# Attention's first chunks in another order: the first r.k group in y's banks, masks ahead of scaling, u's sums one chunk ahead for a while

## The chip, the cores and the metric

The kernel runs on one core of a Trainium2 chip. The metric is device time in microseconds (us) of one execution. The engines of the core run beside each other, each in its own order, and wait for each other by semaphores: TensorE (PE), VectorE (DVE), ScalarE (ACT), GpSimd (POOL) and SyncE (SP), which issues the DMAs.

## What is computed

Three stages follow each other: a linear attention with decay, a mixture of eight experts with a capacity per expert, and a dense MLP with a squared ReLU. The change is in the first stage alone.

```python
def _attn_ref(r, k, v, w, u):            # (4, 8, 768, 48) each; w, u (8, 48)
    state = np.zeros((B, H, D, D))
    for t in range(S):
        kt, vt, rt = (k[:, :, t], v[:, :, t], r[:, :, t])
        cur = np.einsum('bhd,bhe->bhde', u[None] * kt, vt)
        y[:, :, t] = np.einsum('bhd,bhde->bhe', rt, state + cur)
        state = w[None, :, :, None] * state + np.einsum('bhd,bhe->bhde', kt, vt)
    return y

def reference(...):
    x = attention(r, k, v, w, u)         # as 3072 rows of 384
    x = moe(x, w_gate, w1, w2)           # greedy assignment by logit, 384 rows for each expert
    return relu(x @ w_in) ** 2 @ w_out
```

## The kernel before

Attention works on 24 chunks of 128 tokens: chunk n is tokens 128*(n//4) and on of batch n%4, all eight heads at once. So the first four chunks (n < B, B = 4) have no state behind them, and the last four (n >= NCH - B) leave none.

For each chunk two inputs are loaded, `rk` (r and k with channels on partitions, 448 KB) and `tk` (v and k with tokens on partitions, 392 KB). Then these steps follow; each has a function of its name:

- `prep(n)`, line 212, DVE: scales r and k in place by powers of w.
- `prep_rk(n)`, line 216: pr = r*k, on POOL or (argument V) on DVE.
- `ruk(n)`, line 222, PE: eight small products of pr and u, the weight of each token's own term. `ccput(n)`, line 227, DVE: copies that into cc. For most chunks there is no `ruk`; its products ride along in `logits` (line 284) and `ccput` reads them from there.
- `diagonal(n)`, lines 232 and 235, POOL and ACT: makes the matrices AM with cc on the diagonal and zero elsewhere (the masks).
- `qk(n)`, line 246, PE: the products r.k of a chunk, 32 in the trace, into the banks pA0 and pA1. `am(n, s)`, line 250, DVE: copies those above the diagonal into AM by a predicate.
- `state_y` (line 259, from chunk 4 on) and `chunk_y` (line 266), PE: y = r.state + AM.v into the banks pY0 and pY1; `yev`, ACT, copies y out.
- `kvm` (line 326), PE, with `prep_kk` (line 239, POOL) ahead of it: the chunk's part of the state, in bank pk; `tput` adds it.
- `logits(n, m)`, lines 283 and 284, PE: gate logits of chunk n, and in the same bank u's sums of chunk m, so it reads pr of chunk m. `lev`, `by_token`, `logits_by_token`, `lput`, `xput` bring logits and y to tokens and write y to xd in DRAM by DMA.

PSUM has eight banks, one for each of pA0, pA1, pY0, pY1, pk, pt, pl, pm. A second `qk` thus waits until both `am` of the first have read pA. The pr and cc tiles have two buffers, AM three, rk eight and tk six. `unread(n)` issues n products of ones that nobody reads.

Attention is recorded under a manual schedule: each engine gets its instructions in the order in which the code is written. One pass of the loop over n issues the loads of later chunks, `qk(n + 1)`, `am(n + 1)`, y of chunk n and the logits of chunk n - 1. `R.step` and `R.pace` put in pieces of the later routing, from chunk 8 on. In front of the loop a prologue (lines 365 to 386) starts chunks 0 to 3.

Of the kernel before, what the change touches and what calls it, by code (L numbers as in the profile page):

```python
# [25 lines left out]
FT = mybir.dt.float32  # L26
# [8 lines left out]
B, H, S, D = 4, 8, 768, 48  # L35
C = 128
NC = S // C
NCH = B * NC
# [23 lines left out]
def narrow(nc, t, make):  # L62

    if t.dtype != I32:
        return t, []
    V = nc.vector
    low, high, c = t[:, :, 0], t[:, :, 1], []

    def first():
        c.append(make())  # L70
        V.tensor_scalar(c[0], high, 5, 2, op0=OP.logical_shift_left, op1=OP.logical_shift_right)

    return high.bitcast(FT), [
        first,
        lambda: V.scalar_tensor_tensor(c[0], low, 29, c[0], op0=OP.logical_shift_right, op1=OP.bitwise_or),
        lambda: V.scalar_tensor_tensor(high, high, -1073741824, c[0], op0=OP.bitwise_and, op1=OP.bitwise_or)]
# [8 lines left out]
def attention(ctx, tc, a, R, L, xd):  # L85
# [5 lines left out]
    V, G, A_, PE = nc.vector, nc.gpsimd, nc.scalar, nc.tensor  # L91
# [3 lines left out]
    ps = ctx.enter_context(tc.tile_pool(name="aps", bufs=1, space=bass.MemoryType.PSUM))  # L95
# [7 lines left out]
    def load_rk(n):  # L103
        if n < NCH and n not in RK:
            RK[n] = ld.tile([112, 2, 4, 128], FT, name="rk", bufs=8)
            nc.sync.dma_start(flat(RK[n]), a["rk"][n])

    def load_tk(n):
        if n < NCH and n not in TK:
            TK[n] = ld.tile([128, 784], FT, name="tk", bufs=6)  # L110
            nc.sync.dma_start(TK[n], a["tk"][n])
# [26 lines left out]
    def unread(n, name="pt"):  # L138
        trash = ps.tile([128, 512], FT, name=name)
        for _ in range(n):  # L140
            PE.matmul(trash, R.ones, R.warm, start=True, stop=True)
# [55 lines left out]
    def decays_by_token():  # L197
        pt = ps.tile([128, 4, 112], FT, name="pt")
        for i in range(4):
            PE.transpose(pt[:, i, :], TT[:, i, :], ident[:112, :112])  # L200
        kt = KT[:, :384].rearrange("p (i s d) -> p i s d", i=4, s=2)
        for s in range(2):
            A_.activation(kt[:, :, s, :], pt[:, :, half(s)], AF.Copy)


    pr, cc, kks, pA, AM, pYs, pk, pts, pls, lts, pms, tTs = ({} for _ in range(12))

    def v_of(n, h):
        return TK[n][:, 48 * h:48 * h + 64]

    def prep(n):
        V.tensor_tensor(flat(RK[n]), flat(RK[n]), flat(WRK), op=OP.mult)

    def prep_rk(n, eng=G):
        pr[n] = wk.tile([112, 4, 128], FT, name="pr")
        eng.tensor_tensor(pr[n], RK[n][:, 0], RK[n][:, 1], op=OP.mult)

    def ruk(n):

        p = ps.tile([128, 2, 4], FT, name="pm")  # L220
        for i in range(4):
            PE.matmul(p[:, i // 2], pr[n][:, i], Uw[:, i, :4], start=not i, stop=i == 3, skip_group_check=True)
        ccput(n, p)

    def ccput(n, p):
        cc[n] = wk.tile([128, 2, 4], FT, name="cc")
        V.tensor_copy(cc[n], p)

    def diagonal(n):

        AM[n] = wk.tile([128, 4, 2, 128], FT, name="AM", bufs=3)
        G.affine_select(AM[n][:, :2].rearrange("p i s t -> p (i s) t"), cc[n][:, 0, :, None].to_broadcast([128, 4, 128]),
                        pattern=[[0, 4], [1, 128]], compare_op=OP.is_equal, fill=0.0, base=0, channel_multiplier=-1)
        for h in range(4):
            A_.activation(AM[n][:, 2 + h // 2, h % 2], ident, AF.Copy, scale=cc[n][:, 1, h:h + 1])

    def prep_kk(n):
        kks[n] = wk.tile([128, 400], FT, name="kk")
        G.tensor_tensor(kks[n], TK[n][:, 384:784], KT, op=OP.mult)

    def qk(n):
        pA[n] = [ps.tile([128, 4, 128], FT, name=f"pA{s}") for s in range(2)]
        for i in range(4):
            for c in range(2):
                for s in range(2):
                    PE.matmul(pA[n][s][half(c, 64), i], RK[n][half(s), 1, i, 64 * c:64 * c + 64],  # L246
                              RK[n][half(s), 0, i], start=True, stop=True)

    def am(n, s):
        V.copy_predicated(AM[n][:, :, s], mask[:, None, :].to_broadcast([128, 4, 128]), pA[n][s])  # L250
# [11 lines left out]
    def chunk_y(n):  # L262
        c, b = divmod(n, B)
        for i in range(4):
            for s in range(2):
                PE.matmul(pYs[n][s][half(i % 2, 64), i // 2], v_of(n, 2 * i + s), AM[n][:, i, s],  # L266
                          start=not c and i < 2, stop=True, skip_group_check=True)
# [8 lines left out]
    def logits(n, m):  # L276


        p = pls[n] = ps.tile([128, 128], FT, name="pl")
        q = lambda k: p[32 * k:32 * k + 32]  # L280
        for j in range(2):
            for s in range(2):
                PE.matmul(q(2 * s), wg[:, s, j], YT[n % LATE][:, s, j], start=not j, stop=bool(j), skip_group_check=True)  # L283
                PE.matmul(q(2 * s + 1), Uw[:, 2 * s + j], pr[m][:, 2 * s + j], start=not j, stop=bool(j), skip_group_check=True)

    def lev(n):
        lts[n] = wk.tile([128, 128], FT, name="lts")
        A_.activation(lts[n], pls[n], AF.Copy)
# [28 lines left out]
    def kvm(n):  # L317

        c, b = divmod(n, B)
        if c == NC - 1:  # L320
            return
        p = pk[n] = ps.tile([128, 4, 64], FT, name="pk")
        for i in range(4):
            for s in range(2):
                h = 2 * i + s
                PE.matmul(p[half(s, 64), i], kks[n][:, 48 * h:48 * h + 64], v_of(n, h), start=not i, stop=True,  # L326
                          skip_group_check=True)
# [7 lines left out]
    def tput(n):  # L335
        c, b = divmod(n, B)
        if c == 0:
            A_.activation(T[b], pk[n][:112], AF.Copy)
        elif c < NC - 1:
            V.tensor_tensor(T[b], tTs[n], pk[n][:112], op=OP.add)  # L340
# [8 lines left out]
    def early(i):  # L349
        if 0 <= i < NEARLY:  # L350
            tiles[i], todo = narrow(nc, tiles[i], lambda: wk.tile([128, 384], I32, name="c32", bufs=1))
            for f in todo:
                f()
# [10 lines left out]
    ok = lambda n: 0 <= n < NCH  # L364
# [2 lines left out]
    prep(0)  # L367
    prep_rk(0, V)
    prep(1)
    qk(0)  # L370
    ruk(0)
    prep_rk(1, V)
    diagonal(0)
    prep(2)
    unread(2)
    ruk(1)
    decays_by_token()
    unread(3, "pk")
    am(0, 0)
    am(0, 1)  # L380
    diagonal(1)
    prep_rk(2)
    prep_kk(0)
    load_rk(5)
    load_tk(3)
    prep(3)
    for n in range(NCH):
        load_rk(n + AHEAD_RK)
        load_tk(n + AHEAD_TK)
        if n == NCH - B:  # L390
            R.cnt0 = ps.tile([128, 512], FT, name="pk")
        if ok(n - 2):
            lput(n - 2)
            if n - 2 < NCH - LATE:
                xput(n - 2)
            if ok(n + 2):
                ccput(n + 2, pms[n - 2].rearrange("p (s e) -> p s e", s=2)[:, :, 32:36])
        elif n == 1:
            ruk(3)
        if ok(n + 3) and n != 1:  # L400
            prep_rk(n + 3)
        if ok(n + 2) and n:
            diagonal(n + 2)
        if n + 1 < NCH - B:
            prep_kk(n + 1)
        R.pace(n - 1)
        R.step(wide=False)
        fade(n)
        if ok(n + 1):
            qk(n + 1)  # L410
        if ok(n + 4) and n:
            prep(n + 4)
        R.step(wide=False)
        if ok(n + 1):
            am(n + 1, 0)
            R.step(wide=False)
            am(n + 1, 1)
        early(n - NCH + NEARLY)
        R.step(wide=False)
        state_y(n)  # L420
        if ok(n - 1):
            logits(n - 1, min(n + 3, NCH - 1))
            lev(n - 1)
        chunk_y(n)
        yev(n, 0)
        yev(n, 1, None if n < NCH - 1 else V)
        early_split(n - 1 - NCH + NEARLY)
        early_load(n + 2 - NCH + NEARLY)
        kvm(n)
        if n == 0:  # L430
            prep(4)
            ruk(2)
            prep_rk(4, V)
            diagonal(2)
        tput(n)
        if n >= NCH - B:
            R.flush()
        if ok(n - 1):
            if n - 1 < NCH - LATE:
                by_token(n - 1)  # L440
            logits_by_token(n - 1)
        R.step(4)
    n = NCH - 1
    early_split(NEARLY - 1)
    lput(n - 1)
    p = ps.tile([128, E], FT, name="pl")
# [827 lines left out]
```

## Time and profile before

| what | us |
|---|---|
| median of three runs | 792.2 (791.05 to 792.97) |
| the profiled execution | 794.57 |
| its span, first to last instruction | 792.7 |
| PE busy in the span | 764.3 (96%) |
| DVE, ACT, POOL busy | 416.6, 379.3, 301.3 |

A row of the timeline gives the start in us from the span's start, the duration, engine, line, operation, out<-in, shapes and count, and in brackets the idle time of the engine before it with what ended it ("issue" where the profile shows nothing). A row of the windows gives for each engine the busy time in the window and the number of instructions, then the granted clock of TensorE (1.00 is 2.4 GHz, 0.50 is 1.2 GHz), the mean busy share of the 16 DMA engines, and GB/s. In the trace one fp32 product of the program is two weight loads (PEld) and two matmuls (PE), and a transpose one of each.

### The profile page before, as it was taken

To read this page: it belongs to the slowest core of one execution; us is meant where nothing else is said; L and a number is where in the kernel's file an instruction comes from. 1 tells how busy PE (TensorE), PEld (TensorE's weight loads), DVE (VectorE), ACT (ScalarE), POOL (GpSimd) and SP (SyncE) were. 2 spreads that over 40 slices of the span, in tenths; PEclk is the share of its full clock that TensorE was granted. 3 is DMA by queue.
4 is the path that set the end of the run, shared out by engine and by line. 5 is a ranking of instruction groups with operands and counts; after the bars stand their busy time and mean duration, and the time that the engine had idled before them with its cause. 6 is when DMAs were issued, how large, how long until landed. Compare 5 with 4: busy or idle time off the path is not lost.

```text
span 792.7 us, 16726 instructions
## 1 busy us (share of the span) xinstructions
PE 764.3 (96%) x6442; PEld 720.8 (91%) x6443; DVE 416.6 (53%) x1082; ACT 379.3 (48%) x886; POOL 301.3 (38%) x321
## 2 busy tenths in 40 slices
PE   8899997799999999999999999999999999999996
PEld 5688885598999999999999999999999999999996
DVE  8679998988974562356235623562355113212210
ACT  3556661446563464346434643464346445443542
POOL 6879842676754060406040604060406072113001
PEclk8999996899999999999999999999999999999999
DMA  9988761674351050105010501050105042101000
GB/s 212 263 242 255 234 203 55 184 242 143 100 173 47 1 170 1 51 1 170 1 50 1 170 1 50 1 170 1 51 1 170 1 132 58 31 16 35 1 1 30
DMA packets 36591, 73.74 MB, mean 93 GB/s; under 512 B 4657, under 2 KB 24353, under 8 KB 36513
## 3 DMA queue, kind: packets, MB, share of 16 engines
q1 hardware_dynamic: 33440, 63.25, 27.4%
q0 software_dynamic: 3072, 9.44, 3.6%
q8 instruction: 50, 0.82, 0.4%
q14 instruction: 29, 0.23, 0.1%
HBM read 63.24 MB, written 9.44 MB: 92 GB/s over the span
## 4 chain that ended last, share of the span: by engine, by line
PE 86%; DVE 6%; DMA 2%; issue 2%; POOL 1%; ACT 1%; SPq 1%; POOLq 0%; DVEq 0%; ACTq 0%
PE acc L907 12%; PE ph L907 12%; PE acc L909 12%; PE acc L908 12%; PE ph L908 11%; PE ph L909 11%; PE pA L246 3%; PE pY L266 3%; DMA raw<-in_w_dram 2%; PE ph L1033 1%; PE pl L283 1%; PE pt L303 1%; PE pk L326 1%; PE pY L259 1%; PE misc L714 1%
## 5 line engine op out<-in xcount | busy, mean ns | idle before, releaser
L904 POOL TENSOR_TENSOR wl<-raw,wh 128x384 fp32r<-128x384 f32 x114 | 116.0, 1033 | 182.7 <-ACT wh L903 150.8
L1084 DVE TENSOR_TENSOR al<-ph,ah 128x384 fp32r<-128x384 f32 x105 | 58.5, 557 | 148.1 <-ACT ph L1078 146.5
L907 PE MATMUL ph<-YH,wi 128*128 128x384 f32 x384 | 132.7, 346 | 0.0
L908 PE MATMUL ph<-YL,wi 128*128 128x384 f32 x384 | 129.4, 337 | 1.2 <-DVE YL L1057 1.2
L907 PE MATMUL acc<-wo,ah 128*128 128x384 f32 x384 | 130.2, 339 | 0.0
L909 PE MATMUL acc<-wo,al 128*128 128x384 f32 x384 | 128.9, 336 | 0.7 <-POOL al L1084 0.7
L1071 ACT ACTIVATE t<-ph 128x384 f32<-128x384 f32 x128 | 61.6, 487 | 141.5 <-PE ph L909 132.2
L909 PE MATMUL ph<-YH,wi 128*128 128x384 f32 x384 | 128.9, 336 | 0.0
L908 PE MATMUL acc<-wo,ah 128*128 128x384 f32 x384 | 128.6, 335 | 0.0
L1099 POOL DMA_INDIRECT out_dram<-rows,idx x24 | 23.7, 987 | 212.3 <-ACT rows L1097 208.0
L903 ACT ACTIVATE wh<-raw 128x384 fp32r<-128x384 f32 x128 | 66.1, 523 | 72.0 <-DMA raw<-in_w_dram 22.4
L1041 DVE SCALAR_TENSOR_TENSOR al<-ph,ah 128x384 fp32r<-128x384 f32 x64 | 35.6, 556 | 86.7 <-ACT ah L1040 80.1
L908 PEld LDWEIGHTS ph<-YL,wi 128*128 128x128 f32 x384 | 72.2, 188 | 2.2 <-DVE YL L1057 2.0
L909 PEld LDWEIGHTS acc<-wo,al 128*128 128x128 f32 x384 | 72.1, 188 | 1.4 <-POOL al L1084 1.0
L907 PEld LDWEIGHTS ph<-YH,wi 128*128 128x128 f32 x384 | 72.3, 188 | 0.0
L908 PEld LDWEIGHTS acc<-wo,ah 128*128 128x128 f32 x384 | 72.2, 188 | 0.0
L907 PEld LDWEIGHTS acc<-wo,ah 128*128 128x128 f32 x384 | 72.1, 188 | 0.0
L909 PEld LDWEIGHTS ph<-YH,wi 128*128 128x128 f32 x384 | 72.1, 188 | 0.0
L1077 ACT ACTIVATE ah<-t 128x384 fp32r<-128x384 f32 x128 | 67.0, 524 | 2.6
L907 PE MATMUL acc<-ah,wh 128*128 128x384 f32 x192 | 66.3, 345 | 0.0
L909 PE MATMUL acc<-ah,wl 128*128 128x384 f32 x192 | 64.5, 336 | 0.6 <-POOL wl L904 0.6
L908 PE MATMUL acc<-al,wh 128*128 128x384 f32 x192 | 64.3, 335 | 0.0
(255 smaller groups left out, 1511.1 us busy)
## 6 DMA issues: line engine op xcount, KB each, us to landing
raw<-in_w_dram SPq DMA_DIRECT2D x128, 192.0 KB, 2.6
rk<-in_rk_dram SPq DMA_DIRECT2D x24, 448.0 KB, 5.6
tk<-in_tk_dram SPq DMA_DIRECT2D x24, 392.0 KB, 10.7
raw<-in_wi_dram SPq DMA_DIRECT2D x16, 384.0 KB, 3.7
raw<-in_wo_dram SPq DMA_DIRECT2D x16, 384.0 KB, 3.4
xd<-xs SPq DMA_DIRECT2D x24, 192.0 KB, 2.6
rows<-xd,idx POOLq DMA_INDIRECT x24
out_dram<-rows,idx POOLq DMA_INDIRECT x24
```

The source lines that it names most:

```text
L246: PE.matmul(pA[n][s][half(c, 64), i], RK[n][half(s), 1, i, 64 * c:64 * c + 64], RK[n][half(s), 0, i], start=True, stop=True)
L266: PE.matmul(pYs[n][s][half(i % 2, 64), i // 2], v_of(n, 2 * i + s), AM[n][:, i, s], start=not c and i < 2, stop=True, skip_group_check=True)
L903: A_.activation(hi, t, AF.Copy)
L904: (eng or G).tensor_tensor(lo, t, hi.bitcast(FT), op=OP.subtract)
L907: PE.matmul(o, l[0], r[0], start=first, stop=False)
L908: PE.matmul(o, l[0], r[1], start=False, stop=False)
L909: PE.matmul(o, l[1], r[0], start=False, stop=last)
L1041: later(1, lambda: V.scalar_tensor_tensor(hl, o, 0.0, hh.bitcast(FT), op0=OP.max, op1=OP.subtract))
L1071: A_.activation(t, o, AF.Relu)
L1077: A_.activation(gh, t, AF.Square)
L1084: later(2, lambda: (V if p else G).tensor_tensor(gl, t2, gh.bitcast(FT), op=OP.subtract))
L1099: h = G.indirect_dma_start(out=out, out_offset=bass.IndirectOffsetOnAxis(ap=st[p]["idx"][:, i:i + 1], axis=0), in_=t, in_offset=None)
```

## The change

It touches `ruk`, `qk` and the order in `attention`:

- `qk(0)` writes into y's banks (tiles named pY0 and pY1), so `qk(1)` no longer shares banks with it and stands in the prologue, right behind `ruk(0)`. In the loop `qk(n + 1)` is issued from n = 1 on.
- In the prologue `prep(2)` and `prep(3)` move behind the masked copies `am(0)` and `diagonal(1)`; `unread(2)` is gone; the copy of the second u sum stands between the two halves of `am(0)`; `prep_rk(2)` goes from POOL to DVE and `prep_kk(0)` stands ahead of it.
- In the passes n = 1 to 3 `prep` stands behind `am(n + 1)` in place of ahead of it, and pass 2 does two of them. `prep_rk(3)` moves to POOL in pass 1; `prep_rk(4)` on DVE moves to pass 1.
- u's sums: chunks 0, 1, 2 and 5 by `ruk`, chunks 3 and 4 from the logits of chunks 0 and 1 (one pass after these, `far` = 1), from chunk 6 on from the logits four chunks earlier, as before. Before, it was `ruk` for chunks 0 to 3.
- In pass 1 the logits of chunk 0 stand behind y and the state of chunk 1.

```diff
-    def ruk(n):
+    def ruk(n, put=True):
...
-        ccput(n, p)
+        if put:
+            ccput(n, p)
+        return p
...
-    def qk(n):
-        pA[n] = [ps.tile([128, 4, 128], FT, name=f"pA{s}") for s in range(2)]
+    def qk(n, name="pA"):
+        pA[n] = [ps.tile([128, 4, 128], FT, name=f"{name}{s}") for s in range(2)]
...
-    qk(0)
+    qk(0, "pY")
     ruk(0)
+    qk(1)
     prep_rk(1, V)
     diagonal(0)
-    prep(2)
-    unread(2)
-    ruk(1)
+    cc1 = ruk(1, False)
     decays_by_token()
     unread(3, "pk")
     am(0, 0)
+    ccput(1, cc1)
     am(0, 1)
     diagonal(1)
-    prep_rk(2)
+    prep(2)
     prep_kk(0)
+    prep_rk(2, V)
     load_rk(5)
     load_tk(3)
-    prep(3)
     for n in range(NCH):
...
+        far = 1 if n < B else 2
...
-            if ok(n + 2):
-                ccput(n + 2, pms[n - 2].rearrange("p (s e) -> p s e", s=2)[:, :, 32:36])
-        elif n == 1:
-            ruk(3)
-        if ok(n + 3) and n != 1:
-            prep_rk(n + 3)
-        if ok(n + 2) and n:
-            diagonal(n + 2)
+            if ok(n + far):
+                ccput(n + far, pms[n - 2].rearrange("p (s e) -> p s e", s=2)[:, :, 32:36])
+        if n in (1, 3) or ok(n + 3) and n >= B:
+            prep_rk(n + 3 if n > 1 else 3)
+        if n > 1 and ok(n + far):
+            diagonal(n + far)
...
-        if ok(n + 1):
+        if ok(n + 1) and n:
             qk(n + 1)
-        if ok(n + 4) and n:
+        if ok(n + 4) and n >= B:
             prep(n + 4)
...
+        if 0 < n < B:
+            prep(n + (3 if n < 3 else 4))
+        if n == 1:
+            prep_rk(4, V)
+        if n == 2:
+            prep_rk(5)
+            prep(6)
...
-        if ok(n - 1):
-            logits(n - 1, min(n + 3, NCH - 1))
+        def gates():
+            logits(n - 1, min(n + (3 if n > 2 else 2), NCH - 1))
             lev(n - 1)
+
+        if n > 1:
+            gates()
         chunk_y(n)
...
+        tput(n)
         if n == 0:
-            prep(4)
             ruk(2)
-            prep_rk(4, V)
             diagonal(2)
-        tput(n)
+            prep(3)
+        if n == 1:
+            gates()
+        if n == 3:
+            ruk(5)
+            diagonal(5)
```

On PE, at the end of the first u sum in the prologue (pm is u's sum, pt the warming products' bank, pA the r.k of chunk 1):

```order
 L222 MATMUL pm<-Uw,pr 128x4 x4
-L141 LDWEIGHTS onesb
-L141 MATMUL pt<-warmb,onesb 128x512
-L141 LDWEIGHTS onesb
-L141 MATMUL pt<-warmb,onesb 128x512
+L248 MATMUL pA_255<-rk 64x128
+L248 MATMUL pA_256<-rk 64x128
```

The r.k of chunk 1, sixteen products of the program, now fill the place of the two warming products.

On DVE, from the second pr on, through the prologue and the first pass, before (rk<-rk,WRK is the scaling `prep`, AM<-mask the masked copy, cc the copy of u's sum):

```order
L216 TENSOR_TENSOR pr<-rk 112x512
L212 TENSOR_TENSOR rk<-rk,WRK 112x1024
L227 COPY cc<-pm 128x8
L250 COPY_PREDICATED AM<-mask,pA_230 128x4x128
L250 COPY_PREDICATED AM<-mask,pA_231 128x4x128
L212 TENSOR_TENSOR rk<-rk,WRK 112x1024
L250 COPY_PREDICATED AM<-mask,pA_310 128x4x128
L250 COPY_PREDICATED AM<-mask,pA_311 128x4x128
L212 TENSOR_TENSOR rk<-rk,WRK 112x1024
```

and now:

```order
L216 TENSOR_TENSOR pr<-rk 112x512
L252 COPY_PREDICATED AM<-mask,pY_230 128x4x128
L229 COPY cc<-pm 128x8
L252 COPY_PREDICATED AM<-mask,pY_231 128x4x128
L212 TENSOR_TENSOR rk<-rk,WRK 112x1024
L216 TENSOR_TENSOR pr<-rk 112x512
L252 COPY_PREDICATED AM<-mask,pA_255 128x4x128
L252 COPY_PREDICATED AM<-mask,pA_256 128x4x128
L229 COPY cc<-pm 128x8
```

The masked copies of chunk 0 stand ahead of the scaling of chunk 2, and those of chunk 1 ahead of that of chunk 3.

Further on DVE, from the cc copy for chunk 3 on (passes 2 and 3), now:

```order
L229 COPY cc<-pm 128x8
L252 COPY_PREDICATED AM<-mask,pA_449 128x4x128
L252 COPY_PREDICATED AM<-mask,pA_450 128x4x128
L212 TENSOR_TENSOR rk<-rk,WRK 112x1024 x2
L299 TENSOR_REDUCE L<-pm 128x8
L229 COPY cc<-pm 128x8
```

The scalings of chunks 5 and 6 stand in a row behind the masked copies of chunk 3.

On POOL, after the decays' products, before (AM<-cc is the diagonal, kk the state's keys):

```order
L232 AFFINE_SELECT AM<-cc 128x512 x2
L216 TENSOR_TENSOR pr<-rk 112x512
L239 TENSOR_TENSOR kk<-tk,KT 128x400
L216 TENSOR_TENSOR pr<-rk 112x512
L239 TENSOR_TENSOR kk<-tk,KT 128x400
L232 AFFINE_SELECT AM<-cc 128x512 x2
L239 TENSOR_TENSOR kk<-tk,KT 128x400
L216 TENSOR_TENSOR pr<-rk 112x512
L232 AFFINE_SELECT AM<-cc 128x512
```

and now:

```order
L234 AFFINE_SELECT AM<-cc 128x512 x2
L241 TENSOR_TENSOR kk<-tk,KT 128x400 x2
L234 AFFINE_SELECT AM<-cc 128x512
L216 TENSOR_TENSOR pr<-rk 112x512
L241 TENSOR_TENSOR kk<-tk,KT 128x400
L234 AFFINE_SELECT AM<-cc 128x512
L241 TENSOR_TENSOR kk<-tk,KT 128x400
L216 TENSOR_TENSOR pr<-rk 112x512 x2
L234 AFFINE_SELECT AM<-cc 128x512
```

POOL makes pr of chunks 3, 5 and 6 there, the last two in a row, and the diagonal of chunk 4 stands behind them.

## Rows read from the trace of the kernel before

**Rows 1.** The page, chain of work that ended last, shares by engine.
```profile
PE 86%; DVE 6%; DMA 2%; issue 2%; POOL 1%; ACT 1%; SPq 1%; POOLq 0%; DVEq 0%; ACTq 0%
```

**Rows 2.** Windows of attention's start and steady part: engines, granted clock, DMA share, GB/s.
```profile
8.00:46.00 38.00, 33.06 (x583) 27.55 (x586) 26.58 (x41) 18.25 (x59) 26.08 (x22) 0.87 1.00 246
46.00:110.70 64.70, 64.70 (x1535) 55.63 (x1529) 60.58 (x129) 40.24 (x122) 56.35 (x43) 1.00 0.77 235
```

**Rows 3.** The chain in order of time: state products of chunks 5 and 6.
```profile
45.91 0.47 PE pk L326 x14
...
50.11 0.47 PE pk L326 x14
```

**Rows 4.** Timeline of PE: r.k and u's sums of chunks 0 and 1.
```profile
7.98 1.10 PE L246 MATMUL pA<-rk 48*64 48x128 f32 x32 [1.24 <-DVE rk L212]
9.02 1.05 PE L222 MATMUL pm<-Uw,pr 112*128 112x4 f32 x8
...
11.02 1.42 PE L222 MATMUL pm<-Uw,pr 112*128 112x4 f32 x8 [0.71 <-DVE pr L216]
...
14.49 1.99 PE L246 MATMUL pA<-rk 48*64 48x128 f32 x32
```

**Rows 5.** Windows in which the granted clock was half.
```profile
11.50:18.30 6.80, 6.80 (x63) 5.32 (x65) 6.64 (x8) 1.79 (x7) 4.37 (x5) 0.50 1.05 233
...
21.70:25.10 3.40, 3.40 (x54) 2.65 (x48) 2.31 (x3) 1.44 (x5) 3.40 (x3) 0.50 1.04 235
```

**Rows 6.** Timeline of PE: two stops, and the logits of chunk 2 (32.83).
```profile
30.27 0.88 PE L246 MATMUL pA<-rk 48*64 48x128 f32 x23
32.36 0.54 PE L246 MATMUL pA<-rk 48*64 48x128 f32 x9 [1.20 <-issue]
32.83 0.30 PE L283 MATMUL pl<-yt,wg 128*32 128x128 f32 x1
...
37.61 0.32 PE L266 MATMUL pY<-AM,tk 128*64 128x128 f32 x1
40.60 0.99 PE L266 MATMUL pY<-AM,tk 128*64 128x128 f32 x14 [2.67 <-issue]
```

**Rows 7.** Windows between the stops, one before and two after them.
```profile
25.32:32.36 7.04, 5.84 (x134) 4.82 (x131) 4.07 (x8) 5.61 (x17) 5.35 (x6) 1.00 1.03 243
32.36:37.94 5.58, 5.57 (x127) 4.43 (x127) 3.62 (x7) 2.92 (x9) 4.04 (x4) 1.00 1.07 302
37.94:40.60 2.66, 0.00 (x0) 0.00 (x0) 1.12 (x2) 0.28 (x1) 2.01 (x2) 1.00 1.02 306
40.60:45.98 5.38, 5.38 (x127) 4.80 (x129) 3.58 (x7) 2.73 (x9) 2.75 (x3) 1.00 0.74 204
45.98:51.53 5.55, 5.55 (x134) 4.77 (x134) 4.82 (x12) 3.61 (x11) 5.04 (x4) 1.00 0.78 227
```

**Rows 8.** DMA queues, windows 29.5:29.6, 37.7:37.8, 42.3:42.4: packets, MB, share.
```profile
q8 instruction: 1, 0.02, 84.9%
...
q8 instruction: 1, 0.02, 81.2%
...
q8 instruction: 1, 0.02, 77.4%
```

**Rows 9.** Timeline of DVE: pr, a pair of masked copies, two scalings.
```profile
10.19 0.68 DVE L216 TENSOR_TENSOR pr<-rk 112x512 f32<-112x512 f32 x1
...
16.63 1.35 DVE L250 COPY_PREDICATED AM<-mask,pA 128x512 f32<-128x512 int32 x2
17.88 1.30 DVE L212 TENSOR_TENSOR rk<-rk,WRK 112x1024 f32<-112x1024 f32 x1
...
36.16 1.65 DVE L212 TENSOR_TENSOR rk<-rk,WRK 112x1024 f32<-112x1024 f32 x1
```

**Rows 10.** Timelines of ACT and POOL: the masks of chunk 0, pr of chunk 2.
```profile
10.31 1.28 ACT L235 ACTIVATE AM<-ident,cc 128x128 f32<-128x128 f32 x4 [2.26 <-DVE cc L227]
...
13.31 1.27 POOL L216 TENSOR_TENSOR pr<-rk 112x512 f32<-112x512 f32 x1
```

## The prediction

> **What bounds the kernel now.** I read the chain of work that ended last first: TensorE (PE) holds 86% of the span [rows 1]. Then the windows by stage [rows 2]: attention's steady part, 46.00 to 110.70, has PE busy without a gap, and one chunk takes 50.11 - 45.91 = 4.20 us there [rows 3]. What the change leaves alone, from chunk 5 on, is paced by PE, and behind it stand routing and the experts, which start when attention ends. So a microsecond won by the middle of chunk 5 is a microsecond of the total, and only 8 to 46 us is in question: there PE is busy 33.06 of 38.00 us at a mean granted clock of 0.87, with DMA full.
>
> Three things cost time in that stretch. (a) **Order.** The second group of r.k products stands behind the masked copies of chunk 0, since both use pA: the first group runs at 7.98, the second only at 14.49 [rows 4]. (b) **Clock.** The granted clock was 0.50 from 11.50 to 18.30 and again from 21.70 to 25.10 [rows 5], after a PE stretch with a wait of 0.71 us and many four-column products. The 32 products of r.k took 1.99 us at 1.2 GHz and 1.10 us at 2.4 GHz [rows 4]. (c) **Code.** PE stops in the middle of a group at 31.15 for 1.20 us and at 37.94 for 2.67 us, and the profile names no releaser but "issue" [rows 6]. From 32.36 to 37.94 it ran 127 products and 127 weight loads, and from 40.60 to 45.98 127 and 129 [rows 7]: blocks of about 256 instructions each. On the instruction queue a packet of 0.02 MB starts at 29.5, at 37.7 and at 42.3 [rows 8]. The first two start some 2.9 us before the ends of the two stops. So I read the stops as waits for PE's next block of code, asked for when PE enters the block ahead of it, and sent behind other transfers while the DMA engines are full (share 1.03 and 1.07). From block edge to block edge it took 32.36 - 25.32 = 7.04 us and then 40.60 - 32.36 = 8.24 us [rows 7], where PE's own work in a block is 5.4 to 5.6 us. With the share at 0.74 the next block, 40.60 to 45.98, met no stop.
>
> A rule that speaks against this reading: the Trainium skill, Runtime: NRT & Kernel Launch, section Instruction fetch mechanics, says that the sequencer streams blocks of 256 instructions while it executes, and that a block's edge is mostly hidden. The trace agrees on the 256 and not on the hiding, with its 2.67 us; what the rule would make of the time is the first rival.
>
> **The change, part by part.** *r.k of chunk 0 in y's banks, r.k of chunk 1 ahead.* No product is added; two warming products of 512 columns go. The second group follows the first u sum at 10.07 (9.02 + 1.05) and takes 1.10 us, and the second u sum ends at 11.1 + 1.05 = 12.1. PE now has two full groups ahead of 11.5, so I expect the granted clock not to fall there; the cover for this is shown below, because DVE, not PE, sets the pace to 28 us.
>
> *Masks ahead of scaling.* I follow DVE in its new order with the durations of [rows 9]: pr of chunk 1 ends at 10.87 as before; ScalarE's masks of chunk 0 (1.28 us from 10.31 [rows 10]) end at 11.59; the masked copies (1.35 a pair) with the cc copy between them end at 13.0, where the scaling of chunk 2 stood before. Then scaling of chunk 2 (1.65, beside POOL) 14.7, pr 0.6 to 15.3, copies of chunk 1 to 16.6, cc 16.7, scaling of chunk 3 (1.3 to 1.65) 18.2, copies of chunk 2 to 19.5, scaling 4 and pr 4 to 21.4, cc for chunk 3 at 21.6, its masks on ScalarE 1.28 to 22.9, copies to 24.3, scaling of chunks 5 and 6 in a row (2 x 1.3 to 1.65) 26.9 to 27.6. On PE the work beside it needs less: chunk 0's y from 13.3, chunk 1's from 17.7, the r.k of chunk 4 by 25.7. It waits for DVE, so a half clock there costs little.
>
> *u's sums.* Four sums by themselves before and four after (chunks 0, 1, 2, 5 in place of 0, 1, 2, 3), so nothing is added on PE; four ride along with the logits in the same stretch too. But the logits of chunk 2 now need pr of chunk 6, which POOL makes in 1.27 us [rows 10] after that double scaling: 28.2 to 28.9, I take 28.5. Queued behind these logits on PE are chunk 3's y, its state and the y of chunk 4. Before, the same logits ran at 32.83 [rows 6]. So the work alone arrives 4.3 us earlier.
>
> *Moved DMAs.* The first writes to xd and the loads behind them on SP's queue follow the transposes, which come some 4 us earlier; the DMA engines, full at 1.03 to 1.07 [rows 7], get no emptier. The bytes and the packets are the same.
>
> *Code.* The change takes four instructions of warming and a few semaphores out of PE's stream, so the edges stay within six instructions of their place at chunk 4's y. Counted in the new order (each fp32 product is two loads and two products in the trace), the edge that lay in the r.k of chunk 4 now lies in the logits of chunk 2, and the next is a few products into the y of chunk 4, the last at the state product of chunk 5, as before. The first edge is thus entered at 28.5. The work would be at the next after some 7 us (POOL's pr of chunk 7, behind the masks of chunks 4 and 5), about 35.5; a refill in a full queue takes 7.04 to 8.24 us, mean 7.64: 36.1. From there the work is 5.4 us but the refill is again 7.64: 43.8. Before, this edge was at 45.98 [rows 7].
>
> **The sum:** 45.98 - 43.8 = 2.2 us. The 4.3 us that the order wins are thus cut by half, because each block of code comes no faster than DMA lets it. The bounds: two refills at 7.04 give 42.6 and a gain of 3.4; two at 8.24 give 45.0 and a gain of 1.0. I take the mean, since the first of the two refills comes in as full a queue as that of 8.24 and the second when less is left ahead. After 43.8 the next edge needs 5.55 us of work [rows 7] with DMA at 0.78 and should not stop. The profiled execution of 794.57 us (span 792.7 and some 1.9 around it) would become 792.4; it lies 2.4 above the median of the runs, and I take the same 2.2 off that: 792.2 - 2.2 = 790.0.
>
> **Rivals.** *Code is no limit.* If the refills hide, all 4.3 us stay: 787.9. By the skill's rule above this is what happens. For it: from 45.98 on no block stops PE. Against it: both stops with DMA full. *The clock falls in the new wait.* PE would stand from about 41.6 to 43.8. In the trace a wait of 2.67 us at 37.94 left the clock at 1.00, but the drop at 11.50 came after shorter ones. A half-clock stretch as long as 21.70 to 25.10 costs about 1.5 us, since groups stretch there from 1.10 to 1.99. That leaves 0.7: 791.5. The same result would come if the kernel before usually has less half clock than the 10.2 us of this one execution. *Nothing arrives.* DMA alone sets the block edges and the gain is gone by chunk 5: 792.2. *Slower: refills get longer than any shown.* With work running ahead, more loads are in the queue when PE asks, and the price falls on the two refills from 28.5 on. At (45.98 - 28.5) / 2 = 8.74 us each nothing is left; at 9.6 us each the edge is at 47.7 and the kernel 1.7 slower: 793.9. For it: 7.04 grew to 8.24 while the queue stayed full. Against it: fewer bytes are left to load at each edge than the trace's first request had.
>
> **How the numbers follow.** Forecast 0.47 (gain 1.0 to 3.4, three quarters of it over 0.2%, which is 1.6 us and about what a measurement of this kernel can tell from no change); code no limit 0.15; clock 0.20; nothing 0.08; slower 0.10. Faster by over 0.2%: 0.35 + 0.15 + 0.02 of the clock case = 0.52. Slower: 0.10. Within: 0.38. The range reaches from the case without a limit by code, 787.8, to 792.8, past the case of no gain, and leaves out most of the slower case and the extremes.
>
> **What would show it.** Right: the second r.k group near 10.1 and the granted clock 1.00 at 11.5 to 18; the logits of chunk 2 near 28.5 held by POOL's pr; PE stops with "issue" a few products into chunk 4's y (36) and in chunk 5's state product (near 44), longer than the stops of before; 4.2 us a chunk from there on. Wrong: no stop at those edges (then 788), a granted clock of 0.50 after them (then 791 to 792), the logits of chunk 2 later than 30, or a chunk of over 4.2 us after 50.

## The result, and the profile after

The changed kernel is slower: a median of 794.45 us (793.23 to 799.32, 14 runs) against 790.4 us for the kernel before on the same chip (787.88 to 792.97, 14 runs), a ratio of 1.0058 with a 95% interval of 1.0039 to 1.0076. I had forecast 790.0, with 787.8 to 792.8 as the range and one chance in ten for slower. The profiled execution took 796.6 us, its span 794.8. Half of the forecast happened: the work does run ahead up to 27 us. Then it loses all of that and the median loses four microseconds more.

The page's chain by engine answers to [rows 1]:

```profile
PE 83%; DVE 5%; issue 3%; POOL 2%; DMA 2%; ACT 1%; POOLq 0%; SPq 0%; DVEq 0%; ACTq 0%
```

The windows of the changed kernel (busy time of PE, PEld, DVE, ACT and POOL with instruction counts, granted clock, DMA share, GB/s) answer to [rows 2] and [rows 5]:

```profile
8.00:46.00 38.00, 34.69 (x587) 29.71 (x588) 28.73 (x42) 19.81 (x63) 23.06 (x21) 0.82 0.92 250
46.00:110.70 64.70, 64.70 (x1534) 55.67 (x1535) 60.49 (x130) 40.21 (x122) 56.03 (x43) 1.00 0.78 233
8.00:17.40 9.40, 8.57 (x152) 7.37 (x156) 8.36 (x13) 5.64 (x19) 5.38 (x5) 1.00 1.05 292
31.05:41.29 10.24, 10.24 (x123) 9.11 (x122) 7.41 (x10) 4.14 (x13) 5.09 (x6) 0.50 0.84 236
```

By 46 us PE has run 587 products, before it was 583 [rows 2]: by then the kernel is where it was, with more busy time (34.69 against 33.06 us) at a lower clock (0.82 against 0.87). The first half-clock stretch of before, from 11.50, is gone. A new one of 10.24 us stands later, where PE is never idle.

PE's timeline shows how it comes about (line numbers of the changed file are two higher here: L248 is r.k, L286 the u sums in the logits, L268 the y of a chunk):

```profile
7.91 1.10 PE L248 MATMUL pY<-rk 48*64 48x128 f32 x32
8.94 1.05 PE L222 MATMUL pm<-Uw,pr 112*128 112x4 f32 x8
9.93 1.10 PE L248 MATMUL pA<-rk 48*64 48x128 f32 x32
10.96 1.05 PE L222 MATMUL pm<-Uw,pr 112*128 112x4 f32 x8
...
25.95 1.10 PE L248 MATMUL pA<-rk 48*64 48x128 f32 x32
26.98 0.41 PE L285 MATMUL pl<-yt,wg 128*32 128x128 f32 x2
29.86 0.30 PE L286 MATMUL pl<-pr,Uw 112*32 112x128 f32 x1 [2.48 <-POOL pr L216]
...
30.43 1.52 PE L268 MATMUL pY<-AM,tk 128*64 128x128 f32 x16
...
32.73 1.87 PE L222 MATMUL pm<-Uw,pr 112*128 112x4 f32 x8
...
35.55 1.99 PE L248 MATMUL pA<-rk 48*64 48x128 f32 x32
...
39.33 2.03 PE L268 MATMUL pY<-AM,tk 128*64 128x128 f32 x16
...
44.45 1.14 PE L268 MATMUL pY<-AM,tk 128*64 128x128 f32 x16
```

The second r.k group is at 9.93 in place of 14.49 [rows 4]. At the logits of chunk 2 PE stands 2.48 us for POOL's pr of chunk 6. Some 1.2 us after it goes on, the clock falls, and groups that take 1.05, 1.10 and 1.14 us at full clock take 1.87, 1.99 and 2.03. No wait with "issue" is left between 8 and 46 us: the stops for code, on which my sum rested, are not there.

POOL and DVE beside it, around PE's wait and in the slow stretch after it:

```profile
26.50 3.31 POOL L216 TENSOR_TENSOR pr<-rk 112x512 f32<-112x512 f32 x2 [2.11 <-DVE rk L212]
29.77 0.63 POOL L234 TENSOR_SCALAR_AFFINE_SELECT AM<-cc 128x512 f32<-128x512 f32 x1
...
35.54 1.27 POOL L216 TENSOR_TENSOR pr<-rk 112x512 f32<-112x512 f32 x1
36.77 0.63 POOL L234 TENSOR_SCALAR_AFFINE_SELECT AM<-cc 128x512 f32<-128x512 f32 x1
37.37 1.03 POOL L241 TENSOR_TENSOR kk<-tk,KT 128x400 f32<-128x400 f32 x1
```

```profile
25.12 2.35 DVE L212 TENSOR_TENSOR rk<-rk,WRK 112x1024 f32<-112x1024 f32 x2
...
30.43 1.36 DVE L252 COPY_PREDICATED AM<-mask,pA 128x512 f32<-128x512 int32 x2 [2.81 <-POOL AM L234]
...
35.82 2.86 DVE L335 TENSOR_TENSOR tT<-T,W 112x256 f32<-112x256 f32 x1
...
42.68 0.41 DVE L335 TENSOR_TENSOR tT<-T,W 112x256 f32<-112x256 f32 x1
```

POOL makes pr of chunks 5 and 6 in a row, 3.31 us; the first of them lies beside DVE's second scaling, which ends at 27.47. Behind them stands the diagonal of chunk 4, for which DVE's masked copies wait 2.81 us. At 35.82 a small product on DVE (tT, the decayed state) takes 2.86 us where it takes 0.41 otherwise, while POOL runs three instructions in a row from 35.54 to 38.40.

The theories that the runs had to part: the *clock* (PE's new wait lets it fall), *POOL and DVE* (instructions of POOL in a row hold DVE's, and DVE's the rest), and the *base* (the profiled execution of before, from which I took the room for a gain, is not what the kernel before usually does). That the stops with "issue" are waits for PE's code stays a reading: the packets of rows 8 fit it, and no run shows it directly. Letters in an expectation are names for the theories it tells of.

### The profile page after: what moved, and what is told of

It is laid out like the page before. It is cut to its first block, busy times and chain, and to the rows that moved or that the text cites. A ratio compares the mean times of both kernels' runs of the same rounds, so it can differ in the third digit from the quotient of the medians.

```text
span 794.8 us, 16718 instructions
## 1 busy us (share of the span) xinstructions
PE 770.0 (97%) x6440; PEld 725.2 (91%) x6441; DVE 417.9 (53%) x1083; ACT 379.5 (48%) x886; POOL 298.2 (38%) x320
## 4 chain that ended last, share of the span: by engine, by line
PE 83%; DVE 5%; issue 3%; POOL 2%; DMA 2%; ACT 1%; POOLq 0%; SPq 0%; DVEq 0%; ACTq 0%
PE acc L923 12%; PE ph L923 12%; PE acc L925 12%; PE acc L924 12%; PE ph L924 11%; PE ph L925 11%; PE pY L268 3%; PE pA L248 2%; DMA raw<-in_w_dram 2%; PE ph L1049 1%; PE pt L305 1%; PE pl L285 1%; PE pk L328 1%; PE pY L261 1%; PE misc L730 1%
```

## The experiments

All ratios are to the kernel before, run beside them: its median was 790.58 us beside e1 to e4, 791.12 beside e5 to e7, 790.52 beside e8 to e10 and 790.30 beside e11 and e12, each group on another chip. A ratio is not the quotient of the two medians; the two differ by up to 0.17%, so a step of 0.1 or 0.2% between two kernels is no finding by itself. "y3" and "y6" are the starts of chunk 3's and chunk 6's y on PE in the profiled execution, "half" the time at half clock between 8 and 50 us.

| kernel | median us | ratio, 95% interval | y3 | y6 | half | profiled us |
|---|---|---|---|---|---|---|
| before, first profile | 792.2 | | 33.40 | 48.97 | 10.24 | 794.57 |
| after | 794.45 | 1.0058 (1.0039 to 1.0076) | 30.43 | 48.66 | 13.65 | 796.60 |
| e1 before again | 791.41 | 0.9994 (0.9968 to 1.0020) | 31.12 | 48.23 | 6.83 | 793.41 |
| e7 before, third | one run | | 31.64 | 46.39 | 3.41 | 792.84 |
| e2 after again | 795.78 | 1.0052 (1.0026 to 1.0077) | 31.55 | 50.49 | 17.06 | 796.48 |
| e3 after, filled | 792.26 | 1.0012 (0.9990 to 1.0034) | 31.02 | 46.17 | 3.41 | 792.81 |
| e4 banks alone | 790.61 | 1.0004 (0.9981 to 1.0027) | 30.53 | 43.16 | 3.41 | 790.39 |
| e8 banks, filled | 790.85 | 1.0014 (0.9987 to 1.0040) | 30.45 | 44.15 | 0 | 790.61 |
| e5 u undone | 793.46 | 1.0020 (0.9999 to 1.0041) | 33.59 | 47.66 | 10.24 | 792.84 |
| e9 u undone, filled | 791.56 | 1.0017 (0.9995 to 1.0039) | 30.94 | 44.98 | 0 | 790.27 |
| e6 pr 6 on DVE | 792.81 | 1.0011 (0.9990 to 1.0032) | 30.66 | 49.69 | 17.06 | 795.00 |
| e10 pr 6, 7 on DVE, filled | 790.09 | 0.9999 (0.9974 to 1.0024) | 30.00 | 44.12 | 3.41 | 789.23 |
| e11 before, fewer loads ahead | 790.27 | 1.0005 (0.9992 to 1.0018) | 31.81 | 44.43 | 10.24 | 790.31 |
| e12 e10, fewer loads ahead | 789.80 | 0.9995 (0.9981 to 1.0009) | 29.83 | 43.90 | 3.41 | 789.68 |

### Both kernels once more (e1, e7, e2)

No edit.

> The kernel before, unchanged, a second profile. Theory A (the granted clock of TensorE decides, and the profile of before was one with much half clock early): less than 10.2 us at half clock between 8 and 46 us, the edge of 45.98 reached between 43 and 45, ratio 1.000. Theory B (order of VectorE and GpSimd decides, clock a bystander): again about 46.

> The kernel before, a third look. Theory E (the code stops of before depend on how fast DMA moves in this execution: 223 to 241 GB/s from 10 to 30 us in its first profile): with over 260 GB/s from 10 to 30 us the edge into the y of chunk 4 and the next come earlier than 40.6 and 45.98 by 2 us or more. Against E: the same rate and earlier edges, or a higher rate and the same edges.

Of the two stops with "issue" the first was 0.71 us in e1 and 0.86 in e7, the second 2.67 and 1.85; in the first profile they were 1.20 and 2.67 [rows 6]. The rows behind the stops, PE of e1 and then of e7:

```profile
30.08 0.54 PE L246 MATMUL pA<-rk 48*64 48x128 f32 x9 [0.71 <-issue]
...
38.33 0.99 PE L266 MATMUL pY<-AM,tk 128*64 128x128 f32 x14 [2.67 <-issue]
```

```profile
30.60 0.54 PE L246 MATMUL pA<-rk 48*64 48x128 f32 x9 [0.86 <-issue]
...
38.02 0.99 PE L266 MATMUL pY<-AM,tk 128*64 128x128 f32 x14 [1.85 <-issue]
```

The block edge that lay at 45.98 in the first profile came at 45.24 in e1, between what the theories expected, and parted nothing. In e7 it came at 43.40, and the edge of 40.60 at 38.02, both 2.6 us earlier. The windows from 10 to 30 us name a difference, the first profile, e1 and then e7:

```profile
10.00:30.00 20.00, 18.94 (x266) 15.68 (x267) 15.04 (x21) 10.34 (x34) 14.97 (x13) 0.74 1.04 231
```

```profile
10.00:30.00 20.00, 17.68 (x291) 13.97 (x290) 18.15 (x24) 12.13 (x39) 16.75 (x14) 0.91 1.04 263
```

```profile
10.00:30.00 20.00, 17.44 (x289) 14.16 (x288) 18.15 (x24) 11.73 (x38) 16.36 (x14) 0.91 1.05 280
```

At the same busy share of the DMA engines, 1.04 to 1.05, the three executions moved 231, 263 and 280 GB/s. So e7 met what theory E asks for. But e1, also over 260 GB/s, had the second stop at its full 2.67 us and the last edge only 0.74 us earlier, so the rate does not settle it alone. Size and place of the stops, and of the half clock, change from one execution to the next; that both stops are there does not: all three profiles of before have them. In e1 the clock did fall after the 2.67 us stop, for 3.41 us from 39.47; in the first profile the same stop had left it at 1.00.

> The changed kernel, unchanged, a second profile. Theory A: again a PE wait of 2 to 3 us for GpSimd's pr of chunk 6 near 27 to 30, and after it several us at half clock; the later the clock comes back the longer the run; ratio 1.004 to 1.008. Theory B: the y of chunk 4 near 39.5 whether the clock was half there or not.

The loss repeats: 1.0052. The wait for POOL's pr was 3.13 us and the half clock 13.65; it began at 29.71, still in the wait. PE's row and the window of e2:

```profile
30.55 0.42 PE L286 MATMUL pl<-pr,Uw 112*32 112x128 f32 x1 [3.13 <-POOL pr L216]
```

```profile
29.71:43.36 13.65, 12.81 (x151) 11.26 (x153) 8.03 (x10) 4.79 (x16) 7.12 (x8) 0.50 0.83 241
```

Each timed run has a mean granted clock too. Of the 26 runs of the changed kernel in both series, 16 had 0.967 to 0.974, with a median of 796.2 us; the other 10 had 0.979 to 0.983, with a median of 793.4. Of 110 runs of the kernel before beside the experiments, 2 were under 0.975. So most runs of the changed kernel have the fall of the clock, and part of the loss stays without it.

### PE's wait filled (e3)

```diff
+        if n == 3:
+            unread(10)
         if n > 1:
             gates()
```

> The changed kernel with ten warming products of 512 columns (10 x 0.215 us) in the PE wait ahead of the logits of chunk 2. Theory A: the clock stays 1.00 from 27 to 46, the y of chunk 4 comes at about 36 in place of 39.3, 3 to 4 us faster than the changed kernel, ratio 0.997 to 1.003. Theory B: the wait is filled but the y of chunk 4 stays at 38 to 39.5 and the ratio at 1.004 to 1.008.

Ten products that nobody reads now stand ahead of the logits of chunk 2. The same window as of e2, then the wait that is left:

```profile
29.71:43.36 13.65, 13.26 (x264) 10.97 (x263) 11.70 (x16) 7.83 (x25) 9.78 (x11) 1.00 0.74 219
```

```profile
30.45 0.30 PE L286 MATMUL pl<-pr,Uw 112*32 112x128 f32 x1 [0.28 <-POOL pr L216]
```

In the same 13.65 us PE runs 264 products in place of 151, and the median falls from 795.78 to 792.26 on one chip. The y of chunk 4 comes at 36.62 (39.33 in the changed kernel's first profile, 40.97 in e2), as theory A had it. The logits come no earlier (30.45 against 30.55): the filler buys clock alone. So, by the medians, the clock is some 3.5 of the 5.2 us that the changed kernel lost in that series. It is not all: from y3 to y6 e3 takes 15.15 us where three chunks without a wait take 12.62 (e11); 0.92 of that is the u sum of chunk 5, which has its place there now. Its DVE and POOL rows:

```profile
34.78 2.87 DVE L212 TENSOR_TENSOR rk<-rk,WRK 112x1024 f32<-112x1024 f32 x1
...
39.31 2.38 DVE L335 TENSOR_TENSOR tT<-T,W 112x256 f32<-112x256 f32 x1
```

```profile
33.95 0.64 POOL L234 TENSOR_SCALAR_AFFINE_SELECT AM<-cc 128x512 f32<-128x512 f32 x1 [1.95 <-DVE cc L229]
34.55 1.44 POOL L216 TENSOR_TENSOR pr<-rk 112x512 f32<-112x512 f32 x1
35.95 0.63 POOL L234 TENSOR_SCALAR_AFFINE_SELECT AM<-cc 128x512 f32<-128x512 f32 x1
36.55 2.01 POOL L241 TENSOR_TENSOR kk<-tk,KT 128x400 f32<-128x400 f32 x1
38.53 1.27 POOL L216 TENSOR_TENSOR pr<-rk 112x512 f32<-112x512 f32 x1
```

The scaling of a chunk, 1.2 us by itself, takes 2.87, and tT 2.38, while POOL runs one instruction behind the other. Behind them on DVE stand the masked copies; PE waits some 0.4 us for those and 0.2 for POOL's pr of chunk 7. With pr moved from POOL, this should go.

### The parts by themselves (e4, e8, e5, e9)

e4 is the kernel before with the first r.k group in y's banks and nothing else:

```diff
-    qk(0)
+    qk(0, "pY")
     ruk(0)
+    qk(1)
...
-    unread(2)
...
-        if ok(n + 1):
+        if ok(n + 1) and n:
             qk(n + 1)
```

> One part alone: r.k of chunk 0 in y's banks, r.k of chunk 1 in the prologue, two warming products gone; scaling, masks and u's sums as before. Theory A: no new PE wait for GpSimd's pr of chunk 6, no half clock from 30 to 41 because of it; ratio 0.995 to 1.001. If the loss came with the first part (B'): ratio 1.004 or more.

790.61 us and 1.0004: this part costs and brings nothing that can be measured. e8 holds the clock in it by filler products ahead of the state of chunk 0 and of the u sum of chunk 3; against e4:

```diff
+            unread(4)
             ruk(3)
...
+        if n == 0:
+            unread(6)
         kvm(n)
```

> The first part alone (r.k of chunk 0 in y's banks, r.k of chunk 1 in the prologue), with six warming products ahead of the state product of chunk 0 and four ahead of the u sum of chunk 3, where PE waited 1.6 and 0.8 us. Theory A (the clock falls in PE's waits and that costs time for every order, not for the changed one alone): granted clock 1.00 from 8 to 46 us more often, 1 to 2 us below the first part alone, ratio 0.997 to 0.999. If the clock matters only in the changed order: ratio 1.000 as without.

The clock was at 1.00 from 7 to 120 us, and still no gain: 1.0014, where theory A had 0.997 to 0.999. A stop of 0.8 us with "issue" was left in its profile (34.59). The half clock of e4 at 20 us, where PE waits for others anyway, was thus no cost that shows.

e5 is the changed kernel with u's sums as before (chunks 0 to 3 by themselves), so banks and masks are what is left of the change:

```diff
-        far = 1 if n < B else 2
+        far = 2
...
-        if n in (1, 3) or ok(n + 3) and n >= B:
+        if n and ok(n + 3):
...
-            prep(n + (3 if n < 3 else 4))
+            prep(n + (3 if n < 2 else 4))
...
         if n == 1:
             prep_rk(4, V)
-        if n == 2:
-            prep_rk(5)
-            prep(6)
+            prep(5)
...
-            logits(n - 1, min(n + (3 if n > 2 else 2), NCH - 1))
+            logits(n - 1, min(n + 3, NCH - 1))
...
         if n == 1:
+            ruk(3)
+            diagonal(3)
             gates()
-        if n == 3:
-            ruk(5)
-            diagonal(5)
```

> The changed kernel with u's sums as before (own products for chunks 0 to 3, from chunk 4 on with the logits four chunks earlier) and the double scaling one pass earlier; y's banks and masks ahead of scaling kept. Theory C (the loss is the new need of pr of chunk 6 behind a double scaling, with the masks of chunk 4 queued behind it on GpSimd): no PE wait of over 1 us near 27 to 30, y of chunk 4 by 36, ratio 0.995 to 1.001. Theory D (the loss lies in the masks ahead of scaling): ratio 1.004 or more.

1.0020, between what the two theories had, with the y of chunk 4 at 37.80 in place of 36 and 6.83 us of half clock at 24 us behind a wait of 1.6 us. That wait was of my making: a copy that PE needs stood on ScalarE behind the masks of chunk 3. e9 takes it away (the logits ahead of `ruk(3)` and `diagonal(3)`) and fills the gap; against e5:

```diff
         if n == 1:
+            unread(6)
+            gates()
             ruk(3)
             diagonal(3)
-            gates()
```

> The changed kernel with u's sums as before, the logits of chunk 0 ahead of chunk 3's own u sum in pass 1, and six warming products ahead of these logits. Theory C plus A (u's sums and the clock hold the whole loss, masks ahead of scaling cost nothing): clock held, 3 us or more faster than u's sums undone alone, ratio 0.996 to 1.000. Theory D (masks ahead of scaling cost time): ratio still 1.001 to 1.003.

The clock held, and the ratio is 1.0017, in the range of theory D, by which the masks ahead of the scaling cost something by themselves. The trace shows where it could lie. PE of e9, then DVE and POOL:

```profile
35.15 1.15 PE L268 MATMUL pY<-AM,tk 128*64 128x128 f32 x16
...
38.12 0.43 PE L248 MATMUL pA<-rk 48*64 48x128 f32 x2 [0.74 <-DVE AM L252]
...
40.77 1.14 PE L268 MATMUL pY<-AM,tk 128*64 128x128 f32 x16
```

```profile
33.38 2.91 DVE L335 TENSOR_TENSOR tT<-T,W 112x256 f32<-112x256 f32 x1
```

```profile
33.13 1.28 POOL L216 TENSOR_TENSOR pr<-rk 112x512 f32<-112x512 f32 x1 [1.23 <-DVE rk L212]
34.37 0.64 POOL L234 TENSOR_SCALAR_AFFINE_SELECT AM<-cc 128x512 f32<-128x512 f32 x1
34.97 1.04 POOL L241 TENSOR_TENSOR kk<-tk,KT 128x400 f32<-128x400 f32 x1
```

tT is held here too, beside three instructions of POOL, without the new u sums. The masked copies behind it come late, PE waits, and from the y of chunk 4 to that of chunk 5 it takes 5.62 us in place of 4.21 (e11); in e5 it is 5.65. All six profiles with the masks ahead of the scaling and pr of chunk 7 left on POOL (after, e2, e3, e5, e6, e9) have one tT of 2.38 to 2.95 us; in the three of before and in e4, e8 and e11 none is over 0.51. The 1.4 us fit the 0.2% of e5 and e9, but both intervals touch 1.000, so that the 0.2% is time lost is likely and not shown.

By the ratios some 0.2% thus comes with the masks and some 0.3% with u's sums, which bring POOL's two pr in a row and PE's wait for the second. The intervals of e2 (from 1.0026) and of e5 and e9 (up to 1.0041) overlap, so this split is an estimate; that the wait and its half clock cost time is shown by e3, not by it.

### POOL's pr moved to DVE (e6, e10)

e6 makes pr of chunk 6 on DVE (`prep_rk(6, V)` below, and the first line with `n >= B` as it was); e10 that of chunk 7 as well, with the filler of e3. This is e10 against the changed kernel:

```diff
-        if n in (1, 3) or ok(n + 3) and n >= B:
+        if n == 1 or ok(n + 3) and n > B:
             prep_rk(n + 3 if n > 1 else 3)
...
+        if n == 3:
+            unread(10)
         if n > 1:
             gates()
...
+        if n == 2:
+            prep_rk(6, V)
...
             ruk(5)
             diagonal(5)
+            prep_rk(7, V)
```

> The changed kernel with pr of chunk 6 alone moved from GpSimd to VectorE, right behind the double scaling. Theory C: pr of chunk 6 near 28.1 in place of 29.8 and the masks of chunk 4 near 28.8 in place of 30.4, the PE wait about 1 us, the clock held more often, 3 to 5 us faster than the changed kernel, ratio 0.999 to 1.002. Theory D: at most 1 us faster, ratio 1.003 or more.

The wait became 2.44 us, now for DVE, whose pr takes 1.56 us beside POOL's (0.68 by itself [rows 9]):

```profile
29.65 0.42 PE L286 MATMUL pl<-pr,Uw 112*32 112x128 f32 x1 [2.44 <-DVE pr L216]
```

In the profiled execution the clock fell for 13.65 us as in e2, and it took 795.0 us, the slowest of the twelve. The median was 792.81 and the ratio 1.0011, as theory C had it, though the wait did not shrink to the 1 us that it named: seven of the twelve runs had a mean clock of 0.979 or more, and only four of the twelve of e2. So with pr on DVE the fall seems to come less often, and where it comes, as in this profile, it is as long: it matters that PE waits, whoever makes pr.

> The changed kernel with ten warming products ahead of the logits of chunk 2 and pr of chunks 6 and 7 on VectorE in place of GpSimd. Theory F (beside the clock, rows of three and four GpSimd instructions hold VectorE's scaling to 2.9 us in passes 3 to 5): no scaling over 2 us there, y of chunk 6 before 45.5 in place of 46.17, 1 us below the changed kernel with the filled wait, ratio 0.998 to 1.000. Without F: as with the filled wait, 1.001.

790.09 us, 0.9999: with both causes taken away no loss is left to see, and from y3 to y6 it takes 14.12 us in place of 15.15. By time alone e10 cannot be told from e3 (1.0012; the intervals overlap widely), so what POOL's rows cost rests on these starts. DVE's rows of e10, where tT and the scaling took 2.4 to 2.9 us in e3:

```profile
33.79 0.69 DVE L335 TENSOR_TENSOR tT<-T,W 112x256 f32<-112x256 f32 x1
34.40 1.65 DVE L212 TENSOR_TENSOR rk<-rk,WRK 112x1024 f32<-112x1024 f32 x1
```

But no gain appears either, though y3 starts at 30.00.

### Fewer loads ahead (e11, e12)

The last question is where the gain went, and whether PE's stops for code are worth anything. e11 is the kernel before and e12 is e10, each with this edit:

```diff
-    AHEAD_RK, AHEAD_TK = 6, 4
+    AHEAD_RK, AHEAD_TK = 5, 3
```

> The kernel before with its loads issued one chunk later (five chunks of rk and three of tk ahead in place of six and four), nothing else. If the stops with 'issue' in the kernel before come from transfers queued ahead of PE's code (DMA share 1.03 to 1.07 while they last), fewer bytes stand ahead at each request: the stops of 0.7 to 2.7 us near 30 and 36 us shrink to under 0.5, the y of chunk 5 begins at or before 42, and the ratio to before is 0.997 to 1.000. If the loads are what the first chunks wait for, VectorE's scaling waits for rk, the y of chunk 5 comes later than 44, and the ratio is over 1.002.

> The changed kernel with ten filler products ahead of the logits of chunk 2, pr of chunks 6 and 7 on VectorE, and the loads issued one chunk later. If transfers queued ahead are what levels all orders at some 790 us, this one gains over the same without the later loads (790.1 us, ratio 0.9999): the y of chunk 4 begins before 35.7, that of chunk 5 before 39.9, ratio 0.995 to 0.998. If not, or if loads then come too late: 0.999 to 1.003, with the same starts or later ones.

The stops are gone: from 28 to 46 us PE of e11 is busy without a gap, and the y of chunk 5 begins at 40.23 (42.18 to 44.76 in the three profiles of before). The windows of e11, then 8 to 46 us of e10:

```profile
28.00:46.00 18.00, 18.00 (x425) 15.60 (x421) 15.10 (x27) 12.05 (x38) 17.39 (x15) 1.00 0.83 252
```

```profile
8.00:46.00 38.00, 36.79 (x690) 31.06 (x683) 30.81 (x48) 22.27 (x71) 29.51 (x25) 0.87 0.92 247
```

```profile
8.00:46.00 38.00, 36.77 (x700) 30.44 (x702) 33.26 (x52) 22.65 (x71) 26.35 (x22) 0.96 0.95 269
```

And yet the median is that of the kernel before, 790.27 against 790.3, with the narrowest interval of all (0.9992 to 1.0018). This is the miss that explains the most. It supports the base theory: an execution without the stops has y6 at 44.43 and takes 790.31 us, and the kernel before takes 790.3 in the median. Its three profiled executions, which show the stops, took 794.57, 793.41 and 792.84, each 1.7 us or more above the median of the runs beside it. For the kernels whose profile shows neither a stop for code over 0.8 us nor a fall of the clock between 24 and 46 us (e3, e4, e8 to e12) the profiled execution lies between 1.3 below and 0.6 above theirs. Of the 110 timed runs of before beside the experiments only 20 took 792.84 us or more, and all three profiled ones did. So a typical execution of before seems to have little of what I meant to win. This is an inference, since timed runs leave no rows of PE; that taking the profile itself brings the stops of this kernel is a rival that no run tests. The first profile and e11 have the same 10.24 us of half clock, at nearly the same places, and are 4.3 us apart: it is the stops that make the first one long, not its half clock. Later loads are not the only thing that takes the stops away: e4, with the loads as before, shows none.

e12 missed its ratio, 0.9995 against the 0.995 to 0.998 of the theory that loads hold all orders at 790 us. e11 and e10 show what does: between 8 and 46 us PE is busy 36.8 of 38 us in both orders, some 2.3 us of it in e10 with unread products. The three profiles of before had 33.06 [rows 2], 32.93 and 32.99. The five microseconds of idle PE that the change was to fill were those of the profiled executions. In e12 the y of chunk 3 is 2.0 us ahead of e11's (29.83 against 31.81) and the y of chunk 6 only 0.5 (43.90 against 44.43): the u sum of chunk 5 by itself (0.92 us to the next group's start) now stands in the stretch where PE is the bound, and PE waits 0.36 us there for a cc copy. None of these kernels is clearly faster than the kernel before.

## Why the prediction was wrong, step by step

The step that failed is the sum, 45.98 - 43.8. It let two refills of code, 7.64 us each, set the end, and none stopped PE. It put at nothing what did set it: PE's wait of 2.48 us with 10.24 us of half clock behind it (3.5 us by e3) and DVE held by POOL's row (about 1.4 us by e5 and e9). The half clock stood only among the rivals, later and at 1.5 us. And it took its gain off an execution with stops that the median seems not to have.

- **What bounds the kernel: held.** The profiled time less y6 is 745.1 to 746.6 us in all profiles but two, the first of the changed kernel (747.9) and e4 (747.2), where the clock fell once more at the first expert. A microsecond at chunk 6 is one of the total.
- **r.k in y's banks: held, but it brought nothing.** 9.93 for 10.07, and in this profile the clock at 1.00 to 17.4 us; in e2 and e3, with the same order there, it fell at 12.6 and 11.7 us all the same, for 3.41 us. e4 and e8 show no dependence of the time on it.
- **DVE's order: held up to 27 us.** The r.k of chunk 4 stood at 25.95 where I had 25.7, and the double scaling ended at 27.47 where I had 26.9 to 27.6.
- **The logits at 28.5: failed by 1.4 us.** They came at 29.86. I let POOL make one pr in 1.27 us; it makes two in a row there, and the first stands beside DVE's second scaling, so the pair took 3.31.
- **The clock: the rival that came true, priced at less than half.** I put PE's new wait at 41.6 to 43.8 and the price at 1.5 us, and took one row, the 2.67 us stop that left the clock at 1.00, as evidence against it. In e1 the same stop did not. The wait came at 27.4, the fall lasted 10.24 and 13.65 us, and filling it gave back 3.5 us. "A half clock there costs little" was said for the stretch in which PE waits for DVE; this fall began after that stretch, where every row of PE sets the end.
- **The refills of 7.64 us: not the limit.** Nothing stopped PE with "issue" in the changed kernel, so the sum's second half describes a limit that was not met. The rule of the Trainium skill that I had set against it (Runtime: NRT & Kernel Launch, section Instruction fetch mechanics: the edge of a block is mostly hidden) gave the whole 4.3 us as gain; the changed kernel's trace agrees with the hiding, and not with the gain; the three profiles of before disagree with the hiding, by stops of up to 2.67 us.
- **The masks ahead of the scaling, and POOL's row: not priced at all.** I counted DVE's own order and POOL's own order and not what they do to each other. tT's 0.41 us became 2.86 and a scaling's 1.2 became 2.87, while DVE's masked copies, which read their data from PSUM, stayed at 1.33 to 1.38 us. The Trainium skill, SBUF — State Buffer, section "SBUF: two separate sides", says that an operation of DVE with two inputs in SBUF and one of POOL that reads SBUF exclude each other for a whole instruction. The trace agrees on who is held, tT and the scalings but not the copies; it shows more than the rule, since tT waited for three POOL instructions and not for one.
- **The base: failed, as far as the runs tell.** I worked out a gain against the profiled 794.57 and took the same 2.2 us off the median. The gain consisted of stops that all three profiled executions of before have, and the median did not move when e11 took them away. With the base at what e11 shows for an execution without stops, the idle PE between 8 and 46 us is 1.2 us, less than the loss from one wait; half clock is left there as well, and e4 and e8 show no time to be won from it.

Left open: whether a typical execution of the kernel before has the stops in a smaller form or none, and why the runs of the changed kernel whose clock was high are still 3 us over before. The held tT, 1.4 us, and the u sum of chunk 5 in its new place, 0.92 us, may be most of that; e3, whose runs all had a high clock, is 1.7 us over by the medians and 0.9 by its ratio.

## What to carry to other kernels

A profiled execution that is 2 us above the median of the timed ones is not the base for a gain of 2 us. More profiles do not help: here all three had the stops. Take the stops away by an edit that does nothing else, as e11 does, and see whether the median moves before you count on them. Where a change makes PE wait once for 2.5 us in a stretch that PE bounds, count the half clock behind the wait and not only the wait, or keep PE at filler products. And where work is put on POOL in a row, look for the two-input operations that DVE has at that time.

## What was not expected of the hardware

- The wait's price lies behind it: with a wait of PE of 2.44 to 3.13 us (after, e2, e6) came 10.24 to 13.65 us at a granted clock of 0.50, and unread products in its place kept the clock at 1.00 with the same start of the work behind. A stop of 2.67 us left the clock at 1.00 in the first profile of before and was followed by 3.41 us at 0.50 in e1.
- An operation of DVE with two inputs in SBUF took up to seven times as long (0.41 to 2.86 us) beside three POOL instructions in a row.
- At a DMA share of 1.02 to 1.05 the engines moved from 231 to 306 GB/s in different executions and stretches, so that a full share does not tell the rate.
- PE's stops with "issue", up to 2.67 us, were gone from the profile when the loads were issued one chunk later (e11), and the median did not change. They were gone from e4 too, with the loads as before.
